# Window attention and routed experts on one core: a first layer as seven products, part of a table on GpSimd, two weight sums behind a result

## The chip, the cores and the metric

The kernel runs on one core of one Trainium2 chip. The metric is the device time of an execution in microseconds (us); lower is better. Three runs of the kernel before gave 633.9, 635.15 and 629.37 us, so the median is 633.9 us.

## What is computed

The reference is a sliding-window causal attention (8 batches, 8 heads, 576 positions, head width 64, window 64), whose output is the input of a mixture of experts with a "locality gate". Cut to what matters:

```python
# attention: softmax over the 64 keys up to the position, per batch and head
x = attn_out.transpose(0, 2, 1, 3).reshape(8, 576, 512)
logits = x @ w_gate                    # (8, 576, 8 experts)
local = sigmoid(x @ w_local)
for b in range(8):
    for s in range(576):
        fresh_e = argmax(logits[b, s])
        e = fresh_e if s == 0 or local[b, s] < 0.5 else prev_e
        prev_e = e
        p = softmax(logits[b, s])
        h = relu(x[b, s] @ w1[e])      # 512 -> 1024, fp32
        out[b, s] = p[e] * (h @ w2[e]) # 1024 -> 512, fp32
```

## The kernel before, in words

**Attention and first router pass.** Up to about 134 us the kernel computes the attention, 512 tokens at a time, and writes the rows of `x` to memory (`xs`). The routing of the first three sequences is done meanwhile, so that some blocks of tokens are known early.

**Blocks of tokens.** Tokens are sorted by expert into blocks of 256 (two "slots" of 128). For a block, SP loads the expert's weights W1 (2 MB, [128, 4 x 1024]) and W2 (2 MB) into a ring of buffers; GpSimd gathers the rows of `xs` and the softmax weights with indirect DMAs; the block goes through a first layer, a ReLU and a second layer; the result is scaled and scattered to the output rows by GpSimd (L1488). Three first blocks, called -1, -2 and -3, use the early routing. All later blocks need the second router pass, which runs in pieces between the instructions of blocks -1 and -2.

**Seven products.** A block whose `fast1` is set does its first layer (`big_hidden`) as seven products of half size instead of eight. On TensorE (PE) that is 7 x 8 matmuls of 128x128 (L1357). For it VectorE (DVE) makes four sums of the tokens (`xs` in the rows, L1320) and four sums of W1 (L1309, 128x1024 each), ScalarE (ACT) keeps three partial results (L1364), DVE adds them to three quarters (L1369) and ACT does four ReLUs (L1370). A block whose `fast2` is set does its second layer the same way (`big_result`): four sums of W2 (L1320, rows `ws`), four sums of the hidden values (`hs`, L1309), seven products (L1408), three keeps (L1414), three "puts" of a result on DVE (L1419: `put(0,0)`, `put(1,1)`, `put(0,1)`) and one on ACT (L1441). The products share PSUM buffers, so that the seventh product (`hp<-ws,h` in the rows of L1408) waits until `put(1,1)` has read its buffer. `PLAIN1` lists the blocks whose first layer is done directly, by 64 matmuls of 128x256 (L1508) and four ReLUs on ACT (L1521): before, blocks -1 and -2.

**The second router pass** (`Router.second`) is a chain on DVE: counts and ranks of every token, the place of each token (`places`, ending in `lo` at L946 and `hi` at L947), the expert of each block (`experts_of`, `ej`), and then `table`, which turns places into a list of tokens for each slot. `table` handles 37 columns of tokens in pieces of 10, 10, 10 and 7. For a piece, ACT makes `rowh` (one ACTIVATE for each column, L990, and one over the piece, L992), both from `lo`; DVE makes `one` (L980, from `hi`), then `colh`, of which one half is `one * chunk` (L983) and the other `one * posp` (L985); and PE multiplies `rowh` by `colh`, one matmul for a column (L998, 37 in all). From the sum DVE makes the indices for the gathers (L1000 to L1024).

**What sets the order.** Each engine runs its own list in order. The lists of PE and SP are written by hand, by the order of the calls in `run`. There the router is a generator that gives out work at each call of `step`, with `pause` as its account: each `step` takes 1.7 off it, and the next piece comes when it is at zero or below; at i == 1 (block -2) the account is raised by 4.5. Up to block -3 the lists of DVE, ACT and GpSimd are made by a scheduler, from priorities and its own estimates. From the first layer of block -3 on (i == FB-1) all lists are as written. In the loop, `turn` of the next block, with its sums of tokens and of W1, stands ahead of `result` of the present one, so DVE has the four sums of the next W1 ahead of the three puts.

Of the kernel before, what the change touches and what calls it, by code (L numbers as in the profile page):

```python
# [73 lines left out]
MID = (KB, KB - 1)  # L74
PLAIN1, PLAIN2 = (-1, -2), ()

# [636 lines left out]
class Router:  # L713
# [249 lines left out]
    def table(self, psum, cs, ns, lo, hi, idx, gx):  # L963
# [5 lines left out]
        for k in range(0, len(pieces), 2):  # L969
            built = []  # L970
            for b, m in pieces[k:k + 2]:
                rowh = self.oh_p.tile([P, PIECE, P], BF16, name="rowh")[:, :m]
                if ns == FIRST:
# [8 lines left out]
                colh = self.oh_p.tile([P, PIECE, 2, ns], BF16, name="colh", bufs=self.colhs)[:, :m]  # L982
                vec.tensor_tensor(colh[:, :, 0], one, last(self.chunk[:, cs.start + b:cs.start + b + m]).to_broadcast(sh),  # L983
                                  op=Alu.mult)
# [181 lines left out]
class Experts:  # L1166
# [100 lines left out]

    def turn(self, st, quiet, later=False):
        while any(x is st for x, _ in self.asks):
# [21 lines left out]
        if st["fast1"] and not quiet and not later:  # L1291
            self.prepare(st)

    def prepare(self, st):

        st["xq"] = quarters(st["xt"], DK, BIG)
        st["xt"] = self.right("xs", st["xq"])
        w = quarters(st["w1"], DK, F)

        st["wq"] = [[w[0][0], w[1][0]], [w[0][1], w[1][1]]]  # L1300
        st["ws"] = self.left("ws1", st["wq"])

    def left(self, name, a):

        sub, add = Alu.subtract, Alu.add
        s1, s2, s3, s4 = self.sums(name, a)
        for o, x, y, op in ((s1, a[1][0], a[1][1], add), (s2, s1, a[0][0], sub), (s3, a[0][0], a[1][0], sub),
                            (s4, a[0][1], s2, sub)):
            self.nc.vector.tensor_tensor(o, x, y, op=op)  # L1309
        return s1, s2, s3, s4  # L1310

# [20 lines left out]
    def halves(self, st):  # L1332

        hq = st["hq"]
        st["ha"] = [[hq[0][0], hq[1][0]], [hq[0][1], hq[1][1]]]
        st["hs"] = self.left("hs", st["ha"])

    def big_hidden(self, st, step):
# [28 lines left out]
        def relu(o, x, y=None):  # L1367
            if y is not None:
                nc.vector.tensor_tensor(o, x, y, op=add)  # L1369
            nc.scalar.activation(o, x if y is None else o, Act.Relu)  # L1370

# [212 lines left out]
    def run(self, ctx, rt, last=None):  # L1584
# [44 lines left out]
        for i, n in enumerate(order):  # L1629
# [21 lines left out]
            if i == 1:  # L1651
                pause += 4.5
            with tc.issue_after(mark.ins) if i == FB - 1 and mark else nullcontext():
# [10 lines left out]
            if i + 1 == len(order):  # L1664
                self.result(jobs[i], step)
                continue
            self.turn(jobs[i + 1], i + 1 < FB)
            if i + 2 < FB and jobs[i + 1]["fast1"]:
                self.prepare(jobs[i + 1])
            hooks = (step, ) * 6  # L1670
            if order[i + 1] >= KINDS[2]:
# [69 lines left out]
```

## Time and profile before

| what | value |
|---|---|
| median of three runs | 633.9 us (629.37 to 635.15) |
| profiled execution | 631.83 us |
| its span, first to last instruction | 630.1 us |
| mean granted TensorE clock | 0.996 |
| PE busy | 604.0 us, 96% of the span |
| DVE busy | 402.1 us, 64% |
| ACT busy | 200.7 us, 32% |
| GpSimd (POOL) busy | 275.5 us, 44% |
| first layer of block -2 | from 163.94 us |
| first layer of block -3 | from 192.68 us |
| first block of the second pass | from 219.09 us |

The times in the trace are counted from the start of the span. A row of the timeline gives start, length, engine, line, operation, output <- inputs, shape, and how many instructions it joins; in brackets, how long the engine had been idle before it, and what ended that. Instructions of one engine overlap a little (a matmul or a sum that is 1.22 us long may start the next after 1.14 us), so distances from start to start are used as well as lengths.

### The profile page before, as it was taken

To read this page: it belongs to the slowest core of one execution; us is meant where nothing else is said; L and a number is where in the kernel's file an instruction comes from. 1 tells how busy PE (TensorE), PEld (TensorE's weight loads), DVE (VectorE), ACT (ScalarE), POOL (GpSimd) and SP (SyncE) were. 2 spreads that over 40 slices of the span, in tenths; PEclk is the share of its full clock that TensorE was granted. 3 is DMA by queue.
4 is the path that set the end of the run, shared out by engine and by line. 5 is a ranking of instruction groups with operands and counts; after the bars stand their busy time and mean duration, and the time that the engine had idled before them with its cause. 6 is when DMAs were issued, how large, how long until landed. Compare 5 with 4: busy or idle time off the path is not lost. (4 is left out here: it accounts for less than half of the span.)

```text
span 630.1 us, 15072 instructions
## 1 busy us (share of the span) xinstructions
PE 604.0 (96%) x6253; PEld 530.7 (84%) x6253; DVE 402.1 (64%) x757; ACT 200.7 (32%) x368; POOL 275.5 (44%) x261
## 2 busy tenths in 40 slices
PE   8897988999999999999999999999999999999995
PEld 7676766788889998979898889888997998989994
DVE  5667569888986867346472785183927753886730
ACT  3756655632482131203130213022211221213120
POOL 4532111532103567448165873174375765462001
PEclk9999999999999999999999999999999999999998
DMA  8999898886945566487966765678678656965501
GB/s 319 397 419 400 326 377 298 287 319 238 384 154 202 185 227 250 165 295 248 403 244 236 304 221 208 225 305 318 284 262 320 225 186 240 374 217 208 197 18 39
DMA packets 31880, 165.80 MB, mean 263 GB/s; under 512 B 10531, under 2 KB 12217, under 8 KB 22586
## 3 DMA queue, kind: packets, MB, share of 16 engines
q1 hardware_dynamic: 20394, 135.54, 57.9%
q0 software_dynamic: 11408, 29.20, 13.0%
q8 instruction: 51, 0.84, 0.5%
q14 instruction: 27, 0.22, 0.1%
HBM read 145.52 MB, written 19.59 MB: 262 GB/s over the span
## 5 line engine op out<-in xcount | busy, mean ns | idle before, releaser
L1184 POOL DMA_INDIRECT xg<-xs,g x118 | 139.1, 1179 | 46.5 <-issue 25.6
L1488 POOL DMA_INDIRECT out_dram<-y,idx x36 | 40.8, 1133 | 159.0 <-DVE y L1419 69.9
L1408 PE MATMUL hp<-ws,hs 128*128 128x256 f32 x384 | 88.9, 380 | 0.0
L1408 PEld LDWEIGHTS hp<-ws,hs 128*128 128x128 f32 x384 | 72.6, 190 | 10.9 <-issue 1.2
L1357 PE MATMUL hp<-xs,ws 128*128 128x128 f32 x672 | 79.7, 275 | 0.0
L1357 PEld LDWEIGHTS hp<-xs,ws 128*128 128x128 f32 x672 | 77.3, 192 | 0.1
L1508 PE MATMUL hp<-xt,w 128*64 128x64 f32 (+2 forms) x640 | 66.2, 276 | 0.0
L1508 PEld LDWEIGHTS hp<-xt,w 128*128 128x128 f32 (+1 forms) x640 | 60.8, 170 | 4.1 <-issue 0.7
L1419 DVE SCALAR_TENSOR_TENSOR y<-hp,pws,kept 128x256 f32<-128x256 f32 x48 | 22.1, 480 | 63.5 <-issue 38.1
L1408 PE MATMUL hp<-w,h 128*128 128x256 f32 x256 | 60.5, 379 | 0.0
L1369 DVE TENSOR_TENSOR h<-hp,keep 128x512 f32<-128x512 f32 x42 | 28.6, 690 | 44.0 <-PE hp L1357 43.2
L1357 PEld LDWEIGHTS hp<-xt,w 128*128 128x128 f32 x448 | 53.2, 192 | 2.7 <-issue 2.3
L1357 PE MATMUL hp<-xt,w 128*128 128x128 f32 x448 | 54.7, 275 | 0.0
L394 PEld LDWEIGHTS sp<-w 64*64 64x64 f32 x1296 | 39.9, 139 | 16.1 <-issue 11.5
L1408 PEld LDWEIGHTS hp<-w,h 128*128 128x128 f32 x256 | 47.3, 190 | 5.7
L394 PE MATMUL sp<-w 64*64 64x128 f32 (+1 forms) x1296 | 45.8, 272 | 5.7 <-issue 4.2
L425 ACT ACTIVATE p<-sp 128x512 f32<-128x512 f32 x72 | 39.1, 595 | 37.6 <-PE sp L394 35.2
L440 PE MATMUL xo<-vb,p 128*64 128x74 f32 (+1 forms) x576 | 45.0, 230 | 5.5 <-DVE x L450 2.2
L430 DVE TENSOR_TENSOR p<-p,mask 128x1024 f32<-128x1024 f32 x29 | 35.6, 1227 | 22.6 <-ACT p L425 22.5
L1184 POOL DMA_INDIRECT pws<-xw,gx x40 | 43.7, 1093 | 13.1 <-issue 9.8
L440 PEld LDWEIGHTS xo<-vb,p 128*64 128x64 f32 x576 | 39.2, 139 | 9.7 <-issue 4.0
L1320 DVE TENSOR_TENSOR ws<-w 128x1024 f32<-128x1024 f32 x32 | 39.1, 1224 | 11.5 <-PE hp L1408 9.6
(287 smaller groups left out, 967.3 us busy)
## 6 DMA issues: line engine op xcount, KB each, us to landing
w<-in_w_dram SPq DMA_DIRECT2D x22, 2048.0 KB, 9.4
w<-in_w1t_dram SPq DMA_DIRECT2D x20, 2048.0 KB, 8.9
w<-in_kq_dram SPq DMA_DIRECT2D x17, 1024.0 KB, 10.4
w<-in_w_dram SPq DMA_DIRECT2D x24, 512.0 KB, 8.3
xs<-x POOLq DMA_DIRECT2D x9, 1024.0 KB, 7.0
va<-in_v_dram SPq DMA_DIRECT2D x5, 1184.0 KB, 5.3
vtt<-in_vt_dram SPq DMA_DIRECT2D x5, 1024.0 KB, 6.3
va<-in_v_dram SPq DMA_DIRECT2D x3, 1040.0 KB, 14.2
```

What stands on the lines that cost most here:

```text
L394: nc.tensor.matmul(sp[j][c * WIN:(c + 1) * WIN, a:b], lhsT=kt[h, hp, block * WIN:(block + 1) * WIN], rhs=qt[h, hp, a:b], start=not biased, ...
L425: nc.scalar.activation(p[:, j], sp[j], Act.Exp, scale=DH ** -0.5)
L430: masked.append(nc.vector.tensor_tensor(p, p, m.to_broadcast([P, 2, SC]), op=Alu.mult))
L440: nc.tensor.matmul(xo[par * WIN:(par + 1) * WIN, j, s * VW:s * VW + n], lhsT=p[:, j, b * WIN:(b + 1) * WIN], rhs=w[:, s, 2 * hp + j, :n], ...
L1184: return self.nc.gpsimd.indirect_dma_start(out=out, out_offset=None, in_=table[:rows, :], in_offset=bass.IndirectOffsetOnAxis(ap=idx, axis=0))
L1320: self.nc.vector.tensor_tensor(o, x, y, op=sub)
L1357: mm = nc.tensor.matmul(out[:, m, :], lhsT=a[:, kk, m * P:(m + 1) * P], rhs=b[:, kk, :], start=start and m + kk == 0, stop=stop and (m, kk ...
L1369: nc.vector.tensor_tensor(o, x, y, op=add)
L1408: mm = nc.tensor.matmul(out, lhsT=a[:, m, :], rhs=b[:, m, :], start=start and m == 0, stop=stop and m == FK // 2 - 1, skip_group_check=True)
L1419: nc.vector.scalar_tensor_tensor(o, x, pw[i], y2, Alu.mult, Alu.add)
L1488: return self.nc.gpsimd.indirect_dma_start(out=self.out[:, :], out_offset=bass.IndirectOffsetOnAxis(ap=st["idx"][:, s:s + 1], axis=0), in_ ...
L1508: mm = nc.tensor.matmul(hp[a, i, :], lhsT=st["w1"][:, kk, m * P:(m + 1) * P][:, a], rhs=st["xt"][:, kk, :n], start=(kk == 0), stop=(kk == ...
```

## The change

Four edits:

1. `PLAIN1` loses -2. Block -2's first layer is now seven products, with its sums, keeps and adds. With it `relu` in `big_hidden` records its last ACTIVATE, behind which the router puts the second half of each piece's `rowh`; and `pause` is raised by 9.0 instead of 4.5 at i == 1.
2. In `table`, the product `one * chunk` (L983) is issued to GpSimd for the second pass (`ns != FIRST`): four instructions.
3. `left` can make the first two of its four sums and hand back a call that makes the others. `turn` uses it with `rest` for the W1 sums of each block that follows a block of the second kind, from i + 1 = FB on.
4. That call is put into the fifth hook of `big_result`, which stands behind `put(1,1)` and ahead of `put(0,1)`.

```diff
-PLAIN1, PLAIN2 = (-1, -2), ()
+PLAIN1, PLAIN2 = (-1, ), ()
...
-                vec.tensor_tensor(colh[:, :, 0], one, last(self.chunk[:, cs.start + b:cs.start + b + m]).to_broadcast(sh),
+                (vec if ns == FIRST else nc.gpsimd).tensor_tensor(colh[:, :, 0], one, last(self.chunk[:, cs.start + b:cs.start + b + m]).to_broadcast(sh),
                                   op=Alu.mult)
...
-    def turn(self, st, quiet, later=False):
+    def turn(self, st, quiet, later=False, rest=False):
...
         if st["fast1"] and not quiet and not later:
-            self.prepare(st)
-
-    def prepare(self, st):
+            return self.prepare(st, rest)
+
+    def prepare(self, st, rest=False):
...
-        st["ws"] = self.left("ws1", st["wq"])
-
-    def left(self, name, a):
+        st["ws"], later = self.left("ws1", st["wq"], rest)
+        return later
+
+    def left(self, name, a, rest=False):
 
         sub, add = Alu.subtract, Alu.add
         s1, s2, s3, s4 = self.sums(name, a)
-        for o, x, y, op in ((s1, a[1][0], a[1][1], add), (s2, s1, a[0][0], sub), (s3, a[0][0], a[1][0], sub),
-                            (s4, a[0][1], s2, sub)):
-            self.nc.vector.tensor_tensor(o, x, y, op=op)
-        return s1, s2, s3, s4
+        todo = [(s1, a[1][0], a[1][1], add), (s2, s1, a[0][0], sub), (s3, a[0][0], a[1][0], sub), (s4, a[0][1], s2, sub)]
+
+        def make(n):
+            for o, x, y, op in todo[:n]:
+                self.nc.vector.tensor_tensor(o, x, y, op=op)
+            del todo[:n]
+
+        make(2 if rest else 4)
+        return (s1, s2, s3, s4), lambda: make(4)
...
         def relu(o, x, y=None):
             if y is not None:
                 nc.vector.tensor_tensor(o, x, y, op=add)
-            nc.scalar.activation(o, x if y is None else o, Act.Relu)
+            st["last"] = nc.scalar.activation(o, x if y is None else o, Act.Relu)
...
             if i == 1:
-                pause += 4.5
+                pause += 9.0
...
-            self.turn(jobs[i + 1], i + 1 < FB)
+            more = self.turn(jobs[i + 1], i + 1 < FB, rest=i + 1 >= FB and jobs[i]["fast2"])
...
-            hooks = (step, ) * 6
+            hooks = (step, ) * 4 + (more or step, step)
```

**What it moves.** Lines below about L1309 stand six further on in the changed kernel (L1320 is now L1326, L1309 is L1312, L1357 is L1363, L1369 is L1375, L1414 is L1420, L1419 is L1425, L1441 is L1447). On PE, block -2's 32 rows of L1508 give way to the 56 matmuls of L1363, and the 37 matmuls of L998, of which 20 stood between the fourth and the fifth product of block -2's second layer, now stand together behind the seventh, ahead of block -3's first layer. On DVE, the four token sums and four W1 sums of block -2 stand right behind the router's running count (L884) and ahead of block -1's three puts, and most of the router stands behind these puts.

On DVE, in the middle of block -2, the end of the router's `places`. Before, with what follows it (`ws_2803` are the sums of block -2's W2, `hs` those of its hidden values):

```order
L935 TENSOR_REDUCE plc<-pl 128x37
L1144 SCALAR_TENSOR_TENSOR more<-send,more 1x1
L937 MEMSET plc 64x1
L939 MEMSET plc 64x1
L1145 SCALAR_TENSOR_TENSOR ej<-bend,more 1x1
L941 CAST plc_i<-plc 128x37
L943 TENSOR_SCALAR lo_i<-plc_i 128x37
L944 TENSOR_SCALAR plc_i<-plc_i 128x37
L946 CAST lo<-lo_i 128x37
L947 CAST hi<-plc_i 128x37
L1320 TENSOR_TENSOR ws_2803<-w 128x1024 x2
L1320 TENSOR_TENSOR ws_2803<-w,ws_2803 128x1024
```

The same place in the changed kernel:

```order
L935 TENSOR_REDUCE plc<-pl 128x37
L1312 TENSOR_TENSOR hs<-h 128x512 x2
L1312 TENSOR_TENSOR hs<-hs,h 128x512
L937 MEMSET plc 64x1
L939 MEMSET plc 64x1
L1312 TENSOR_TENSOR hs<-h,hs 128x512
L941 CAST plc_i<-plc 128x37
L960 TENSOR_REDUCE ef<-ec 1x43
L943 TENSOR_SCALAR lo_i<-plc_i 128x37
L1142 TENSOR_SCALAR more<-qend 1x1
L961 TENSOR_SCALAR ej<-ef 1x43
L944 TENSOR_SCALAR plc_i<-plc_i 128x37
```

`lo` and `hi` follow within four rows. Before, they stood ahead of the four sums of W2 and of the four `hs`; now the four W2 sums, the three adds of the first layer and all four `hs` stand ahead of them.

On ACT, in block -2's second layer (`kept` is what it keeps of the products, `h` the plain first layer's ReLU), one piece of the difference:

```order
+L1420 ACTIVATE kept_2862<-hp,pws 128x256
 L990 ACTIVATE rowh<-io_744,lo 128x128 x4
-L1521 ACTIVATE h<-hp 128x512
-L990 ACTIVATE rowh<-io_744,lo 128x128 x7
+L1420 ACTIVATE kept_2868<-hp,pws 128x256
+L990 ACTIVATE rowh<-io_744,lo 128x128 x5
+L1420 ACTIVATE kept_2874<-hp,pws 128x256
+L990 ACTIVATE rowh<-io_744,lo 128x128 x2
 L992 ACTIVATE rowh<-rowh,ones 128x1280
```

All `rowh` stood between the ReLUs of block -2's first layer and its second layer's keeps; now the first of them stands behind the first keep, and the last (not shown) behind the result on ACT.

On DVE, between two later blocks, as it repeats from there on (`ws_3341` are the next block's W1 sums, L1419 the three puts, `ws_3408` the W2 sums). Before:

```order
L1309 TENSOR_TENSOR ws_3341<-w 128x1024
L1309 TENSOR_TENSOR ws_3341<-ws_3341,w 128x1024
L1309 TENSOR_TENSOR ws_3341<-w 128x1024
L1309 TENSOR_TENSOR ws_3341<-w,ws_3341 128x1024
L1419 SCALAR_TENSOR_TENSOR y<-hp,pws,kept_3356 128x256
L1419 SCALAR_TENSOR_TENSOR y<-hp,pws,kept_3363 128x256
L1419 SCALAR_TENSOR_TENSOR y<-hp,pws,kept_3370 128x256
L1320 TENSOR_TENSOR ws_3408<-w 128x1024
```

In the changed kernel:

```order
L1312 TENSOR_TENSOR ws_3383<-w 128x1024
L1312 TENSOR_TENSOR ws_3383<-ws_3383,w 128x1024
L1425 SCALAR_TENSOR_TENSOR y<-hp,pws,kept_3396 128x256
L1425 SCALAR_TENSOR_TENSOR y<-hp,pws,kept_3403 128x256
L1312 TENSOR_TENSOR ws_3383<-w 128x1024
L1312 TENSOR_TENSOR ws_3383<-w,ws_3383 128x1024
L1425 SCALAR_TENSOR_TENSOR y<-hp,pws,kept_3410 128x256
L1326 TENSOR_TENSOR ws_3450<-w 128x1024
```

Two sums of 128x1024 have moved from ahead of the first two puts to behind them. On GpSimd the four new products stand between the second scatter of block -1 and the first of block -2; SP's list is the same.

More of the change, by code (lines that the diff above doesn't have):

```diff
@@ L1335, in halves @@
         st["ha"] = [[hq[0][0], hq[1][0]], [hq[0][1], hq[1][1]]]
-        st["hs"] = self.left("hs", st["ha"])
+        st["hs"], _ = self.left("hs", st["ha"])
     def big_hidden(self, st, step):
```

## The prediction

> **What bounds the kernel now.** I read the page's busy times first, then PE's timeline around the blocks that change, then what PE waits for there and later.
>
> ```profile
> PE 604.0 (96%) x6253; PEld 530.7 (84%) x6253; DVE 402.1 (64%) x757; ACT 200.7 (32%) x368; POOL 275.5 (44%) x261
> ```
>
> PE works 96% of the span: matmuls taken from it, or a wait of PE taken away or added, show in the time; another engine matters only where PE waits for it. PE from the end of block -1's second layer to the start of block -3's first:
>
> ```profile
> 162.11 1.99 PE L1408 MATMUL hp<-ws,h 128*128 128x256 f32 x8 [0.44 <-DVE y L1419]
> 163.94 13.98 PE L1508 MATMUL hp<-xt,w 128*128 128x256 f32 x64
> 177.75 1.04 PE L1279 MATMUL tp<-ident,xg 128*128 128x128 f32 x8
> ...
> 191.75 0.99 PE L998 MATMUL r<-colh,rowh 128*128 128x108 bf16 x17
> 192.57 0.27 PE L168 MATMUL yp<-ident,ok 128*1 128x128 f32 x1
> 192.68 1.95 PE L1357 MATMUL hp<-xt,w 128*128 128x128 f32 x16
> ```
>
> The one gap shown is 0.44 us ahead of the seventh product at 162.11, where DVE is late with a put. The table's matmuls (L998) wait for nothing. So PE bounds this stretch, but DVE is close behind it:
>
> ```profile
> 152.97 0.53 DVE L884 TENSOR_TENSOR_SCAN run<-te,zero 128x184 f32<-128x184 f32 x1
> ...
> 161.58 0.47 DVE L1419 SCALAR_TENSOR_TENSOR y<-hp,pws,kept 128x256 f32<-128x256 f32 x1
> ```
>
> ```profile
> 146.30:156.00 9.70, 9.70 (x51) 8.44 (x50) 9.13 (x27) 2.63 (x6) 1.90 (x2) 1.00 0.81 273
> 153.40:178.00 24.60, 24.16 (x114) 20.92 (x113) 24.25 (x93) 10.26 (x29) 6.20 (x6) 1.00 0.90 327
> ```
>
> The fields of the windows are the stretch, its length, busy time of PE, PEld, DVE, ACT and POOL, the granted clock (1.00), the DMA share and GB/s. From 153.4 to 178 DVE is busy 24.25 of 24.6 us: what is put ahead of something in its list delays it by its own length.
>
> **Seven products for block -2 (edit 1), on PE.** In the first block of the second pass PE's groups start at:
>
> ```profile
> 207.01 1.89 PE L1408 MATMUL hp<-w,h 128*128 128x256 f32 x8
> ...
> 219.09 1.95 PE L1357 MATMUL hp<-xt,w 128*128 128x128 f32 x16
> ...
> 231.60 1.89 PE L1408 MATMUL hp<-w,h 128*128 128x256 f32 x8
> ```
>
> Seven products of a first layer take 231.60 - 219.09 = 12.5 us, against 177.75 - 163.94 = 13.8 for the plain one: **-1.3 us**. A second layer takes 219.09 - 207.01 = 12.1. On ACT three keeps are added, where it was busy 10.26 of 24.6 us and now has its rowh later: nothing.
>
> **The same edit on DVE.** Four token sums and four W1 sums now stand right behind L884, ahead of block -1's puts. Their lengths, from a later block:
>
> ```profile
> 368.45 0.41 DVE L1320 TENSOR_TENSOR xs<-xt,xs 128x256 f32<-128x256 f32 x1
> 368.78 1.21 DVE L1309 TENSOR_TENSOR ws<-w 128x1024 f32<-128x1024 f32 x1
> ...
> 373.45 1.26 DVE L1419 SCALAR_TENSOR_TENSOR y<-hp,pws,kept 128x256 f32<-128x256 f32 x3
> 376.40 1.23 DVE L1320 TENSOR_TENSOR ws<-w 128x1024 f32<-128x1024 f32 x1 [1.70 <-PE hp L1408]
> ```
>
> Four token sums at 0.33 to 0.41 make 1.5 us, the W1 sums 373.45 - 368.78 = 4.7: 6.2 us. In return most of the router moves behind the put at 161.58. Of the 8.1 us between 153.5 (end of L884) and 161.58 some 3 stay ahead (down to the ranks), an estimate from the order, so the put would start at 153.5 + 6.2 + 3 = 162.7, 1.1 us later. The sums can also wait for block -2's W1, four parts that SP issued from 146.28 on (its row stands below). The window from 146.3 to 156 moved 9.7 x 273 = 2.65 MB, W1's 2.1 and two gathers among it, so I take 156 for W1, up to 1 us of waiting behind the token sums. The put is 1 to 2 us late; I take 1.5. Block -2's first layer then starts at 165.5 and ends at 178.0, against 177.75: the late put uses up what the seven products give.
>
> **The table (edits 1 and 2) decides.** `lo` was there at 167.4 (first row of ACT's chain below). Now the token and W1 sums (6.2), the W2 sums (4.7, of the same size), three adds and four hs stand ahead of it:
>
> ```profile
> L1369 DVE TENSOR_TENSOR h<-hp,keep 128x512 f32<-128x512 f32 x42 | 28.6, 690 | 44.0 <-PE hp L1357 43.2 <-ACT h L1370 0.7
> L1309 DVE TENSOR_TENSOR hs<-h 128x512 f32<-128x512 f32 x32 | 22.0, 688 | 9.9 <-ACT h L1370 9.7
> ```
>
> 3 x 0.69 = 2.1 and 4 x 0.69 = 2.75; 15.7 us in all, so `lo` at 183.1. A wait for W1 adds up to one; neighbours overlap (the W1 sums start 1.17 us apart and are 1.21 long), which takes about one. The other bound is the first layer: its sixth product ends at 165.5 + 6 x 1.79 (a seventh of 12.5) = 176.2, then come its add, its ReLU, the hs and six small rows: not before about 181. I take **182.1**, bounds 181 and 184. Behind `lo` stands ACT's chain:
>
> ```profile
> 167.42 1.28 ACT L990 ACTIVATE rowh<-io,lo 128x128 bf16<-128x128 f32 x4 [2.81 <-DVE lo L946]
> ...
> 169.09 2.14 ACT L990 ACTIVATE rowh<-io,lo 128x128 bf16<-128x128 f32 x7
> 171.13 1.35 ACT L992 ACTIVATE rowh<-rowh,ones 128x1280 bf16<-128x1280 bf16 x1
> 172.38 0.58 ACT L1521 ACTIVATE h<-hp 128x512 f32<-128x512 f32 x1
> ...
> 188.40 1.04 ACT L992 ACTIVATE rowh<-rowh,ones 128x896 bf16<-128x896 bf16 x1
> ```
>
> One L990 takes (171.13 - 169.09) / 7 = 0.29 us, 37 take 10.8; L992 takes 172.38 - 171.13 = 1.25 three times and 1.04 once, 4.8; two keeps and block -2's result stand between, half as wide as L1521's 0.58 us, some 0.37 each, 1.1, an estimate. Sum 16.7 us: the last rowh is ready at 182.2 + 16.7 = 198.9. Before, the chain began at 167.42, with 25 us until PE took its last piece, and cost nothing.
>
> PE comes to L998 early: transposes at 178.0 for some 0.9, second layer to 178.9 + 12.1 = 191.0. There it waits, and behind the last rowh it still has seven matmuls of (192.57 - 191.75) / 17 = 0.05 and L168's 0.11, and some 0.2 for the signal. Block -3's first layer, queued behind them, starts at 198.9 + 0.2 + 0.35 + 0.1 = 199.6 instead of 192.68: **+6.9 us**. This holds the -1.3 and the late put, which end at the same place. With the bounds of `lo` it is +5.8 to +8.8.
>
> What else is late: SP's next weights wait for `ej`, now at about 182.5.
>
> ```profile
> 146.28 17.33 SPq L1261 DMA_DIRECT2D w<-in_w_dram  x16
> ...
> 177.94 12.62 SPq L1261 DMA_DIRECT2D w<-in_w_dram  x2
> ```
>
> W1 of the first block of the second pass was issued at 177.94 and is 5 us late at 183, for a first layer that was at 219.09 and comes at 226: hidden. The gathers come behind the table as before and move with it.
>
> **GpSimd's four products.** DVE loses them behind `lo`, where the chain is ACT's: no gain. No two-input GpSimd operation is in the trace; nearest are one-input copies:
>
> ```profile
> L369 POOL COPY vb<-va 64x1184 f32<-64x1184 f32 x5 | 6.2, 1246 | 50.5 <-PE xo L440 39.1 <-ACT vb L355 11.3
> ```
>
> ```profile
> 19.79 2.04 POOL L373 COPY vb<-va 64x1040 f32<-64x1040 f32 x1
> ```
>
> 1246 ns for 1184 elements, 1.05 ns each, gives 0.6 us for 540; the slowest, 1.96 ns, doubled for two inputs, 2.1 us. I take 1.3, between them. They start at 183.3 with the first `one`, end between 185.7 and 191.7, and are needed by 199: nothing, up to 3.9 us each. Were rowh early again, they would be due by 191, and at 2.1 us each cost up to 1 us.
>
> The Trainium skill ("GPSIMD Engine Reference", section 3.1, "Elementwise — side-by-side cycle accounting") gives 4497 ns for a two-input addition of 2048 elements; for 540 that makes 1.2 us, an estimate, and leaves the sum as it is.
>
> **W1's last sums behind the second put (edits 3 and 4).** In later blocks PE waits for the same put; from 206 to 625 us its waits read:
>
> ```profile
> PE hp L1408 <- DVE y L1419: 1.6, 5, 0.4
> ```
>
> ```profile
> 372.18 1.89 PE L1408 MATMUL hp<-w,hs 128*128 128x256 f32 x8
> 374.37 1.99 PE L1408 MATMUL hp<-ws,h 128*128 128x256 f32 x8 [0.30 <-DVE y L1419]
> ```
>
> The seventh product starts 2.19 us behind the sixth, where 12.1 / 7 = 1.73 is the rule: 0.46 each, five times **-2.3 us** (at least the row's 1.6). Two W1 sums, 2.3 us, go behind the put, which can start at about 372 instead of 373.9. What comes late: `put(0,1)`, by these sums to about 374.5, when its own product has just ended; the next first layer, which takes the two sums in its fifth and sixth product, 7 us in; the W2 sums, ahead of which DVE stood idle 1.70. All hidden; if not, the 2.3 us are lost, and up to as much again if PE then waits for the two sums in full.
>
> **Sum.** +6.9 - 2.3 = +4.6 us on the profiled 631.83: 636.4. The median is 2.1 above that execution: **638.4 us**.
>
> **The rivals.** *The give-back fails* (chance 0.17): the table waits, but each removed put wait comes back, by `put(0,1)`, the W1 sums or a transfer that PE now meets earlier. For it: each wait was only 0.46 us, and the next may be as close. Against it: the 1.70 us of idle DVE. +6.9 alone: 640.8, slower.
>
> *GpSimd decides the table* (0.10): its products take over 3.9 us each, with repeated operands and bf16, which no row shows. At 5 us they end at 203.4, some 4.4 behind the rowh: 642.8, slower. Against it: this is over twice the dearer bound.
>
> The Trainium skill ("SBUF — State Buffer", section "Who interferes with whom") says that a DVE instruction with two SBUF inputs and a GpSimd one that reads SBUF shut each other out. From 182 on DVE has 1.5 us of token sums, 4.7 of W1 sums, three puts and the table's own rows; with GpSimd's 5.2 us one after the other that leaves some 4 us for puts and table rows until 199, so by this rule little is added. No row here shows it yet.
>
> *The table is not late* (0.15), the other side: `lo` comes by 174, and rowh is done by 191. Then the late put (+1.5), -1.3 and -2.3 remain: -2.1, 631.8. For it: rowh had 25 us to spare. Against it: `hs`, ahead of `lo`, needs the sixth product, which ends at 176.
>
> *W1 is later than 156* (0.05): at 160 the late put, `lo` and rowh all move by 4, since DVE's list stands behind its sums: 642.4, slower. For it: the DMA share of 0.90. Against it: by bytes it is there.
>
> **How the numbers follow.** The forecast has 0.53, its own range 636 to 641. A measurement of this kernel tells about 1% (6.3 us) from no change: below 627.6 or above 640.2. Faster: 0.05, a third of the not-late case, with a lower draw (the three runs spread by 5.8). Slower: 0.10 of the forecast's 0.53 (the upper bound of `lo`), 0.10 of the failed give-back, 0.09 and 0.04 of GpSimd and W1: 0.33. Within 1%: 0.62. The range 631 to 644 takes in both sides' cases.
>
> **What would show it.** Right: block -2's L1363 from 165 to 166; `lo` at 181 to 184 and rowh from there for 17 us without a gap; PE some 7 us idle at L998, released by ACT's L992; block -3's first layer at 199 to 200; past 206 no wait of the seventh product on DVE's `y`. Wrong: PE's gap at L998 put down to `colh`; `lo` below 175; the later blocks' wait still there, or another in its place.

## The result and the profile after

Four runs each, in turn on one chip: 639.54 us for the changed kernel (638.48 to 642.1), 631.68 for the one before (629.37 to 635.15). The ratio is 1.015, 95% interval 1.012 to 1.018: slower by 1.5%, some 9.5 us (the two medians lie 7.9 us apart), where +4.6 had been forecast. The page of the profiled execution, the slowest of the four:

```profile
span 640.2 us, 15191 instructions
PE 604.6 (94%) x6301; PEld 533.5 (83%) x6301; DVE 409.8 (64%) x764; ACT 203.3 (32%) x371; POOL 279.9 (44%) x265
```

PE is busy as long as before (604.6 against 604.0 us) in a span that is 10.1 us longer: most of the loss is waiting. (The seven products should have taken 1.3 us from PE's busy time; slow matmuls, below, put it back.) PE from block -1's transposes to block -3's:

```profile
150.40 1.04 PE L1279 MATMUL tp<-ident,xg 128*128 128x128 f32 x8
...
163.21 1.99 PE L1414 MATMUL hp<-ws,h 128*128 128x256 f32 x8 [1.42 <-DVE y L1425]
165.04 1.95 PE L1363 MATMUL hp<-xt,w 128*128 128x128 f32 x16
...
177.54 1.04 PE L1279 MATMUL tp<-ident,xg 128*128 128x128 f32 x8
...
191.62 2.84 PE L1414 MATMUL hp<-ws,h 128*128 128x256 f32 x8 [2.68 <-DVE y L1425]
194.25 1.97 PE L998 MATMUL r<-colh,rowh 128*128 128x108 bf16 x20
198.62 0.66 PE L998 MATMUL r<-colh,rowh 128*128 128x108 bf16 x10 [2.40 <-ACT rowh L992]
201.46 0.81 PE L998 MATMUL r<-colh,rowh 128*128 128x108 bf16 x7 [2.18 <-ACT rowh L992]
202.06 0.42 PE L168 MATMUL yp<-ident,ok 128*1 128x128 f32 x1
202.28 3.62 PE L1363 MATMUL hp<-xt,w 128*128 128x128 f32 x16
...
217.41 1.04 PE L1279 MATMUL tp<-ident,xg 128*128 128x128 f32 x8
```

The first layer of block -2 starts at 165.04 and ends at 177.54, about as forecast (165.5, 178.0). Block -3's starts at 202.28, not at 199.6. Two things here had not been in the sum: the seventh product of block -2 waits 2.68 us for a put, and block -3's first product takes 205.69 - 202.28 = 3.41 us where one takes 1.79. DVE in between:

```profile
181.27 0.16 DVE L946 CAST lo<-lo_i 128x37 f32<-128x37 int32 x1
...
183.25 0.61 DVE L985 TENSOR_SCALAR colh<-one,posp 128x540 bf16<-128x540 bf16 x2
183.80 0.70 DVE L980 TENSOR_TENSOR one<-ios,hi 128x540 bf16<-128x540 f32 x1
185.49 1.42 DVE L980 TENSOR_TENSOR one<-ios,hi 128x378 bf16<-128x378 f32 x1 [0.99 <-POOL colh L983]
186.84 1.50 DVE L985 TENSOR_SCALAR colh<-one,posp 128x540 bf16<-128x540 bf16 x2
188.26 0.71 DVE L1326 TENSOR_TENSOR xs<-xt,xs 128x256 f32<-128x256 f32 x1
...
191.09 0.47 DVE L1425 SCALAR_TENSOR_TENSOR y<-hp,pws,kept 128x256 f32<-128x256 f32 x1
```

```profile
182.71 5.98 POOL L983 TENSOR_TENSOR colh<-one,chunk 128x540 bf16<-128x540 bf16 x4 [8.18 <-DVE one L980]
```

The same four products, each in a row of its own (views of the short windows in which they run):

```profile
182.71 2.74 POOL L983 TENSOR_TENSOR colh<-one,chunk 128x540 bf16<-128x540 bf16 x1 [8.18 <-DVE one L980]
185.42 1.08 POOL L983 TENSOR_TENSOR colh<-one,chunk 128x540 bf16<-128x540 bf16 x1
186.47 1.39 POOL L983 TENSOR_TENSOR colh<-one,chunk 128x540 bf16<-128x540 bf16 x1
187.83 0.87 POOL L983 TENSOR_TENSOR colh<-one,chunk 128x378 bf16<-128x378 bf16 x1
```

`lo` comes at 181.27 (forecast 182.1). Then GpSimd's four products take 6.0 us, and beside them the fourth `one` waits 0.99 us for a product to free its buffer and takes 1.42 us, two scales take 1.50 where two took 0.61 just before, and a token sum 0.71 where one takes 0.42. The second put, behind all this, two more token sums and a W1 sum, starts at 191.09. ACT, whose rowh were to set the time:

```profile
181.47 1.28 ACT L990 ACTIVATE rowh<-io,lo 128x128 bf16<-128x128 f32 x4 [0.60 <-DVE lo L946]
...
194.50 0.47 ACT L1447 ACTIVATE y<-hp,pws 128x256 f32<-128x256 f32 x1 [2.94 <-PE hp L1414]
194.87 2.44 ACT L990 ACTIVATE rowh<-io,lo 128x128 bf16<-128x128 f32 x8
...
200.36 1.04 ACT L992 ACTIVATE rowh<-rowh,ones 128x896 bf16<-128x896 bf16 x1
```

ACT stands idle for 2.94 us in the middle of the chain: its next instruction is block -2's result, which needs the late seventh product, and fourteen columns of rowh are queued behind it. Without that gap the chain takes 17.0 us (181.47 to 201.40, less 2.94), where the prediction had 16.7. And the granted clock (the field behind the five busy times):

```profile
191.60:194.30 2.70, 2.68 (x9) 2.03 (x10) 2.70 (x4) 0.00 (x0) 0.00 (x0) 0.69 0.93 394
194.30:202.30 8.00, 3.42 (x40) 3.08 (x39) 1.06 (x1) 6.87 (x17) 1.75 (x1) 0.71 0.26 107
202.30:205.70 3.40, 3.40 (x18) 3.40 (x18) 3.26 (x16) 0.00 (x0) 0.00 (x0) 0.50 0.00 0
```

It was 1.00 up to 191.6; after PE's gap of 2.68 us it is 0.69, so that the seventh product takes 2.84 us instead of 1.99, and for 3.4 us of full work from 202.3 on it is 0.50. From block -3's first product to the transposes behind its first layer it is 217.41 - 202.28 = 15.1 us; before it was 206.13 - 192.68 = 13.45. So the idle time cost 1.7 us more after it had ended (that the idle time is the cause is shown by the runs on the clock below). In the later blocks the wait for the put is gone:

```profile
PE hp L1363 <- DVE h L1375: 0.4, 2, 0.2
```

That is all PE waits for from 206 to 640 us; before, the five put waits stood beside it. By PE's starts: from block -3's transposes to the first layer of the last block 623.63 - 217.41 = 406.2 us, before 615.09 - 206.13 = 409.0, so -2.7 us.

```profile
615.09 3.95 PE L1508 MATMUL hp<-xt,w 128*64 128x64 f32 x128
```

```profile
623.63 3.95 PE L1514 MATMUL hp<-xt,w 128*64 128x64 f32 x128
```

The attention before block -1 takes a different time in each execution (its transposes start between 147.0 and 151.2 us in the runs below), and so does the end (14.0 to 16.7 us from the last block's first layer). So I compare stretches between these marks. The change adds 11.1 us up to block -3's transposes and gives back 2.7: +8.4, which is within the interval of the ratio (7.5 to 11.4 us).

### The profile page after: what moved, and what is told of

It is laid out like the page before. It is cut to its first block, busy times and chain, and to the rows that moved or that the text cites. A ratio compares the mean times of both kernels' runs of the same rounds, so it can differ in the third digit from the quotient of the medians.

```text
span 640.2 us, 15191 instructions
## 1 busy us (share of the span) xinstructions
PE 604.6 (94%) x6301; PEld 533.5 (83%) x6301; DVE 409.8 (64%) x764; ACT 203.3 (32%) x371; POOL 279.9 (44%) x265
## 5 line engine op out<-in xcount | busy, mean ns | idle before, releaser
L1184 POOL DMA_INDIRECT xg<-xs,g x118 | 134.5, 1140 | 47.7 <-issue 23.8
L1414 PE MATMUL hp<-ws,hs 128*128 128x256 f32 x384 | 88.8, 380 | 0.0
L1363 PE MATMUL hp<-xs,ws 128*128 128x128 f32 x720 | 85.8, 276 | 0.0
L1363 PEld LDWEIGHTS hp<-xs,ws 128*128 128x128 f32 x720 | 83.2, 193 | 0.2
L1414 PEld LDWEIGHTS hp<-ws,hs 128*128 128x128 f32 x384 | 72.6, 190 | 10.9 <-issue 1.2
L1425 DVE SCALAR_TENSOR_TENSOR y<-hp,pws,kept 128x256 f32<-128x256 f32 x48 | 23.1, 481 | 65.7 <-issue 41.2
L1363 PEld LDWEIGHTS hp<-xt,w 128*128 128x128 f32 x480 | 58.7, 197 | 2.8 <-issue 2.3
L1414 PE MATMUL hp<-w,h 128*128 128x256 f32 x256 | 60.5, 379 | 0.0
L1363 PE MATMUL hp<-xt,w 128*128 128x128 f32 x480 | 60.2, 280 | 0.0
L1375 DVE TENSOR_TENSOR h<-hp,keep 128x512 f32<-128x512 f32 x45 | 30.6, 689 | 45.7 <-PE hp L1363 45.7
L1514 PE MATMUL hp<-xt,w 128*64 128x64 f32 (+2 forms) x576 | 52.2, 264 | 0.0
L1414 PEld LDWEIGHTS hp<-w,h 128*128 128x128 f32 x256 | 47.3, 190 | 5.7
L1184 POOL DMA_INDIRECT pws<-xw,gx x40 | 45.3, 1132 | 14.2 <-issue 8.5
L430 DVE TENSOR_TENSOR p<-p,mask 128x1024 f32<-128x1024 f32 x29 | 37.1, 1279 | 21.6 <-ACT p L425 21.5
L1514 PEld LDWEIGHTS hp<-xt,w 128*128 128x128 f32 (+1 forms) x576 | 48.6, 168 | 2.5 <-issue 0.7
L1376 ACT ACTIVATE h<-h 128x512 f32<-128x512 f32 x45 | 28.3, 632 | 64.3 <-DVE h L1375 64.3
## 6 DMA issues: line engine op xcount, KB each, us to landing
va<-in_v_dram SPq DMA_DIRECT2D x3, 1040.0 KB, 15.3
```

The lines of the kernel that those rows point to most:

```text
L430: masked.append(nc.vector.tensor_tensor(p, p, m.to_broadcast([P, 2, SC]), op=Alu.mult))
L1184: return self.nc.gpsimd.indirect_dma_start(out=out, out_offset=None, in_=table[:rows, :], in_offset=bass.IndirectOffsetOnAxis(ap=idx, axis=0))
L1363: mm = nc.tensor.matmul(out[:, m, :], lhsT=a[:, kk, m * P:(m + 1) * P], rhs=b[:, kk, :], start=start and m + kk == 0, stop=stop and (m, kk ...
L1376: st["last"] = nc.scalar.activation(o, x if y is None else o, Act.Relu)
L1414: mm = nc.tensor.matmul(out, lhsT=a[:, m, :], rhs=b[:, m, :], start=start and m == 0, stop=stop and m == FK // 2 - 1, skip_group_check=True)
L1425: nc.vector.scalar_tensor_tensor(o, x, pw[i], y2, Alu.mult, Alu.add)
```

## The experiments

Twelve kernels. The table gives PE's starts in us behind the start of block -1's transposes (L1279), so that differences ahead of it drop out; "rest" is from block -3's transposes to the last block's first layer; the ratio is to the kernel before, timed in turn on the same chip.

| run | first layer of -2 | `lo` | transposes of -2 | first layer of -3 | transposes of -3 | rest | ratio (95%) |
|---|---|---|---|---|---|---|---|
| before | 13.7 | 17.0 | 27.5 | 42.4 | 55.9 | 409.0 | 1 |
| the change | 14.6 | 30.9 | 27.1 | 51.9 | 67.0 | 406.2 | 1.015 (1.012 to 1.018) |
| rest_only | 13.7 | 16.9 | 27.5 | 42.4 | 55.9 | 406.1 | 0.993 (0.990 to 0.995) |
| no_seven | 13.7 | 16.9 | 27.5 | 42.4 | 55.9 | 406.0 | 0.995 (0.992 to 0.998) |
| no_gpsimd | 14.8 | 31.1 | 27.4 | 49.0 | 63.8 | 406.1 | 1.008 (1.005 to 1.011) |
| lo_first | 15.3 | 24.3 | 28.3 | 50.0 | 64.8 | 406.1 | 1.007 (1.005 to 1.010) |
| y_on_dve | 15.7 | 32.8 | 29.4 | 51.0 | 66.4 | 406.1 | 1.013 (1.009 to 1.017) |
| keep_warm | 14.8 | 31.1 | 27.3 | 53.9 | 67.4 | 406.2 | 1.016 (1.013 to 1.019) |
| lo_first_dve | 14.3 | 23.1 | 27.1 | 45.0 | 59.6 | 406.0 | 1.001 (0.999 to 1.004) |
| all_three | 17.2 | 26.5 | 30.5 | 48.1 | 61.6 | 406.1 | 1.003 (1.000 to 1.005) |
| late_table | 13.7 | 21.3 | 27.5 | 45.2 | 59.6 | 419.6 | 0.999 (0.995 to 1.002) |
| free_all | 14.3 | 23.3 | 27.3 | 43.4 | 58.3 | 423.4 | 0.998 (0.994 to 1.001) |
| best | 13.1 | 22.5 | 26.6 | 42.9 | 57.5 | 418.6 | 0.998 (0.995 to 1.001) |
| keep_warm2 | 16.0 | 32.8 | 29.4 | 50.8 | 64.3 | 419.1 | 1.004 (1.000 to 1.008) |

The last four ran on a chip where every kernel was slower, the one before too (644.6 us): the rest took 419 to 423 us, with waits that the other traces do not show. Of these runs the stretches up to block -3 are compared with the others, the totals only among themselves. The line numbers differ a little from run to run: L1423 in some of the rows below is L1414 of the change, L1456 is L1447, L1364 is L1363.

### The parts of the change, each without the other

`rest_only`, edits 3 and 4 alone:

```diff
-PLAIN1, PLAIN2 = (-1, ), ()
+PLAIN1, PLAIN2 = (-1, -2), ()
...
-                (vec if ns == FIRST else nc.gpsimd).tensor_tensor(colh[:, :, 0], one, ...
+                vec.tensor_tensor(colh[:, :, 0], one, ...
...
-                pause += 9.0
+                pause += 4.5
```

> Edits 3 and 4 alone (W1's last two sums behind the second put), with block -2's plain first layer and the table product on DVE as before. Theory A (the three parts add: the late put wait of later blocks is gone, about -2.7 us by the starts of the later blocks in the two traces): ratio to before 0.995 to 0.997, no wait of L1414 on DVE y past 206 us, block -3's first layer near 192.7. Rival B (the waits come back elsewhere, and the later part only looked faster because it ran at another place): ratio 1.000, and another wait of about 0.5 us in each of five blocks.

Up to block -3 every mark stands as before to 0.1 us; the rest is 2.9 us shorter, and PE waits for no put. Theory A holds, and B falls. The ratio is somewhat better than the 2.9 us (0.995) that the trace shows; its interval just reaches that.

`no_seven` takes back edit 1 alone (the first and the last hunk above), with the products on GpSimd.

> The change without edit 1: block -2's first layer plain, the four table products on GpSimd, W1's last sums behind the second put. Theory A (the late lo makes the loss; GpSimd costs only where DVE's delay reaches PE): lo near 167, rowh early, block -3's first layer within 1 us of 192.7, ratio to before 0.994 to 0.998. Rival C (GpSimd's products and DVE shutting each other out are the main loss): block -3 starts 3 us late or more, ratio at least 1.001. In either case DVE's one and colh rows beside the four products should be up to twice as long as before.

As theory A had it, block -3 starts at 42.4, as before. Yet DVE was disturbed here too:

```profile
175.50 3.21 POOL L983 TENSOR_TENSOR colh<-one,chunk 128x540 bf16<-128x540 bf16 x3
179.21 0.86 POOL L983 TENSOR_TENSOR colh<-one,chunk 128x378 bf16<-128x378 bf16 x1 [0.50 <-DVE one L980]
```

```profile
176.66 2.47 DVE L980 TENSOR_TENSOR one<-ios,hi 128x378 bf16<-128x378 f32 x1 [1.14 <-POOL colh L983]
...
188.99 0.48 DVE L1425 SCALAR_TENSOR_TENSOR y<-hp,pws,kept 128x256 f32<-128x256 f32 x1 [0.64 <-ACT rowh L990]
```

The `one` of 378 takes 2.47 us, over four times its 0.54 in the kernel before, where at most twice had been expected. But DVE has idle time left ahead of the second put (0.64 us), so nothing arrives at PE. A disturbance of this kind costs nothing here and 2.9 us in the change: what decides is the cover, the time that DVE has to spare ahead of the put.

`no_gpsimd` takes back edit 2 alone (the second hunk).

> The change with the four table products back on DVE. Theory A (late lo is some 7 us; GpSimd adds by a chain: DVE late, second put late, seventh product late, ACT's result copy late, the last rowh behind it late): lo still at 181 to 182, but ACT's rowh without the 2.9 us gap ahead of block -2's result, block -3's first layer at 199 to 200 instead of 202.3, ratio to before 1.007 to 1.011. Rival C (GpSimd is the main loss): block -3 at 195 or earlier, ratio below 1.003. Rival D (GpSimd costs nothing, since the chain is ACT's anyway): block -3 at 202, ratio 1.015.

```profile
192.49 0.46 ACT L1447 ACTIVATE y<-hp,pws 128x256 f32<-128x256 f32 x1
```

```profile
200.25 3.49 PE L1363 MATMUL hp<-xt,w 128*128 128x128 f32 x16
```

ACT's result has no idle time ahead of it, and block -3 starts at 49.0 behind the mark: +6.6 against before (forecast +6.9), and 2.9 earlier than in the change. Theory A holds: the late table is 6.6 us, edit 2's part 2.9, through the put. The first product is slow here too (3.33 us until the next).

The run does not hold all else fixed, though: DVE's order changed with it. Here the second put stands ahead of three token sums and a W1 sum, in the change behind them. From `lo` to the second put it is 6.95 us here (182.30 to 189.25) and 9.82 in the change (181.27 to 191.09). By the rows, the four products that left DVE's list give back some 2.4 us, the four sums that came ahead of the put take some 2.1, and DVE's wait and its long rows beside GpSimd make some 3.0. So the 2.9 us are the price of edit 2 with the order that came with it; no run separates the two. Some 0.85 of them, an estimate, is the slow clock, since ACT's result starts only when the seventh product, 0.85 us longer than usual, has ended.

### The late `lo`

`lo_first` runs the router on, at the end of block -2's first layer, until `lo` and `hi` are issued, and puts the W2 sums and hs behind them:

```diff
-        self.prepare2(st)
+        if not link:
+            self.prepare2(st)
...
-        self.halves(st)
+        marks = []
+        if link:
+            old = link[1]()
+            while link[1]() is old or len({id(x) for x in link[1]()}) > 1:
+                step()
+            marks = [x.ins for x in link[1]()]
+            self.prepare2(st, marks)
+        with self.tc.issue_after(marks[-1]) if marks else nullcontext():
+            self.halves(st)
```

> The change, with the router run on until lo and hi ahead of block -2's four W2 sums and four hs sums on DVE (these are put behind hi in the order); everything else as in the change, GpSimd's products too. Theory A: lo near 173, rowh starts 8 us earlier, so the wait at L998 is gone or under 4 us, block -3's first layer at 194 to 198 instead of 202.3; ratio to before 1.000 to 1.007. Rival C (GpSimd's products hold the put, and the put holds everything): the seventh product still waits about 2.7 us, and block -3 stays above 200; ratio above 1.010.

`lo` is 6.6 us earlier behind the mark, block -3 only 1.9: the ratio is as theory A had it, the gain behind the mark is not. The seventh product still waits 2.39 us for its put, as rival C had it, ACT's result waits 4.46 for the seventh product, and seven columns stand behind it. With `lo` early, the other chain decides. `lo_first_dve` takes GpSimd's products away as well:

> The change with lo and hi ahead of block -2's W2 sums and hs sums, and the table products on DVE: both causes of the late table taken away, but ACT's result copy still stands ahead of the last seven rowh columns. Theory A: second put on time to half a microsecond, block -3's first layer about 45 us behind block -1's transposes (42.4 before, 51.9 in the change), ratio to before 0.995 to 1.003. Rival G (seven products in block -2 cost by DVE's full list whatever the order): block -3 48 us or more behind them, ratio 1.006 or more.

Block -3 at 45.0, ratio 1.001: both as theory A had them, G falls. What is left is this:

```profile
189.49 0.48 ACT L1456 ACTIVATE y<-hp,pws 128x256 f32<-128x256 f32 x1 [0.87 <-PE hp L1423]
```

```profile
193.26 0.64 PE L998 MATMUL r<-colh,rowh 128*128 128x108 bf16 x7 [2.36 <-ACT rowh L992]
```

PE waits 2.36 us for the last seven columns. They stand behind the result in ACT's list, and ACT could begin them only when PE had ended the second layer.

### What holds the last columns

`y_on_dve`: the change, with block -2's result quarter on DVE, so that it is out of ACT's list.

```diff
-        nc.scalar.activation(y[1][:, :w], px, Act.Copy, scale=pw[1])
+        if st.get("ydve"):
+            nc.vector.tensor_scalar(y[1][:, :w], px, pw[1], None, Alu.mult)
+        else:
+            nc.scalar.activation(y[1][:, :w], px, Act.Copy, scale=pw[1])
...
+                jobs[1]["ydve"] = True
```

> The change, with the last quarter of block -2's result scaled on DVE instead of ACT, so that no rowh stands behind it on ACT; GpSimd's products, the late lo and the late second put stay as in the change. Theory A (GpSimd's products reach the time through one chain: DVE late, second put late, seventh product late, ACT's result copy late, the last fourteen rowh columns late): rowh without a gap on ACT, last L992 at about 198 instead of 201.4, block -3's first layer some 3 us earlier after the same start, ratio to before 1.007 to 1.011, as with the products on DVE. Rival E (the late seventh product itself is what costs): block -3 within 1 us of the change's, ratio 1.013 to 1.017.

In this execution block -2 started 1.1 us later than in the change: its W1 sums waited 0.92 us for the weights instead of 0.33, and behind the longer wait for the put (1.98 us) block -1's seventh product took 2.56 us instead of 1.99. Behind block -2's transposes, block -3 starts 21.7 us, as in no_gpsimd (21.7) and 3.1 less than in the change (24.7): the chain through ACT is as theory A says. The ratio, 1.013, is the one that rival E had named, but it holds the late start too, so it does not tell the theories apart. And one wait took the removed one's place:

```profile
196.61 0.40 ACT L990 ACTIVATE rowh<-io,lo 128x128 bf16<-128x128 f32 x1 [0.55 <-PE r L998]
```

The first column of the fourth piece waits for PE's matmuls of the first: rowh has three buffers, and a fourth piece needs one back. `all_three` puts both together, the early `lo` with the products on DVE and the result on DVE:

> As the run with lo first and the products on DVE, and block -2's last result quarter on DVE as well. Theory A: the last rowh is ready before PE has finished block -2's second layer, PE idle at L998 under 1 us, block -3's first layer 42 to 43.5 us behind block -1's transposes, ratio to before 0.990 to 0.997, which is that of W1's last sums alone, give or take the 1.3 us of the seven products. Rival G: no better than the run without this, ratio 1.000 or more.

Missed: block -3 at 48.1 and the ratio 1.003 are what rival G had named, and behind block -2's transposes block -3 starts hardly earlier than in `lo_first_dve` (17.7 us against 17.9). W1 came late here (1.98 us of waiting, block -2 started at 17.2), and PE still waited for the last columns:

```profile
193.56 2.15 ACT L990 ACTIVATE rowh<-io,lo 128x128 bf16<-128x128 f32 x7 [1.35 <-PE r L998]
```

```profile
196.84 0.51 PE L998 MATMUL r<-colh,rowh 128*128 128x108 bf16 x7 [2.35 <-ACT rowh L992]
```

So there is a third cause, which I had not seen: in the change all 37 table matmuls stand behind the seventh product, so the first piece's buffer comes free only then, and the last piece takes ACT 3.2 us from there (193.56 to 196.79 here). `late_table` gives this order to `rest_only`, by one number:

```diff
-                pause += 4.5
+                pause += 9.0
```

> The kernel with only W1's last sums moved (edits 3 and 4) and one number of edit 1: the router's account raised by 9.0 instead of 4.5, which on PE puts all 37 table matmuls behind the seventh product of block -2's second layer (20 stood behind its fourth product); the plain first layer, the early lo and the products on DVE stay. Theory H (rowh has three buffers, so the fourth piece's rowh waits until PE has taken the first piece, and then still needs 3.2 us on ACT): block -3's first layer starts 1.5 to 3 us later, at 44 to 45.5 us behind block -1's transposes instead of 42.4, with PE waiting on ACT's L992 ahead of the last seven matmuls; ratio to before 0.995 to 0.999, against 0.993 for the sums alone. Rival: the order on PE is free as long as lo is early: 42.4 to 43, ratio 0.993.

```profile
188.79 0.47 ACT L1447 ACTIVATE y<-hp,pws 128x256 f32<-128x256 f32 x1 [2.05 <-PE hp L1414]
```

```profile
192.56 0.81 PE L998 MATMUL r<-colh,rowh 128*128 128x108 bf16 x7 [2.35 <-ACT rowh L992]
```

As theory H had it, block -3 is at 45.2, +2.8, with the plain first layer and `lo` at 21.3 (4.4 later, by the same number, but ACT was idle 2.05 us ahead of the result, so `lo` was not what held it). This run alone does not tell the buffer from ACT's list: the seven columns stand right behind the result and start as it ends (189.28), about when PE has taken the first piece. `all_three`, with the result off ACT, still had the wait; `free_all` gives it a fourth buffer for `rowh` and for `one`, and a fifth for `colh`:

```diff
-        rt.rows_of(ctx, tc, "rt_oh2", 3)
+        rt.rows_of(ctx, tc, "rt_oh2", 4)
```

> As the run all_three, with four buffers for rowh and one instead of three. Theory H: the wait of 2.35 us for the last rowh piece is gone, since no rowh waits for PE any more; block -3's first layer starts 14 to 15 us behind block -2's transposes (17.7 with three buffers), ratio to before 0.993 to 0.999, held above that of the sums alone by block -1's late put where W1 lands late. Rival G (seven products in block -2 cost by DVE's full list whatever the order): 17 us or more, ratio 1.002 or more.

```profile
193.81 0.51 PE L998 MATMUL r<-colh,rowh 128*128 128x108 bf16 x7 [0.75 <-ACT rowh L992]
```

No rowh waits for PE, and the wait at L998 falls from 2.35 to 0.75 us. Block -3 starts 16.1 us behind block -2's transposes (17.7 with three): better, short of the 14 to 15 expected, because ACT's own work still ends last. G, which had 17 us or more and a ratio of 1.002 or more, falls. Its transposes stand at 58.3 all the same, since PE then waits 1.61 us for DVE's `t` at L1022. `best` also moves block -2's W1 sums behind block -1's second layer in the program:

```diff
-            if i + 2 < FB and jobs[i + 1]["fast1"]:
-                self.prepare(jobs[i + 1])
             hooks = (step, ) * 4 + (more or step, step)
...
             self.result(jobs[i], step, hooks)
+            if i + 2 < FB and jobs[i + 1]["fast1"]:
+                self.prepare(jobs[i + 1])
```

> As free_all, with block -2's W1 sums made in the program behind block -1's second layer, so that the order puts only two of them ahead of its first two puts. Theory A and H together: block -1's seventh product waits under 0.7 us for its put, block -2's first layer starts 13.5 to 14.2 us behind block -1's transposes also where W1 lands late, and what the seven products save (1.3 us) is left: block -3's first layer 41 to 42.5 us behind block -1's transposes, ratio to before 0.990 to 0.994, at or below that of the sums alone. Rival: a new wait in block -2's first layer for the W1 sums that are now later, ratio 0.996 or more.

Missed, by 0.4 us in block -3's start and in the ratio (0.998 for 0.990 to 0.994). The put is no longer late: block -2's first layer at 13.1, its transposes at 26.6, 0.9 us ahead of before. But block -3 starts at 42.9, and its transposes stand at 57.5 against 55.9 before:

```profile
192.35 0.51 PE L998 MATMUL r<-colh,rowh 128*128 128x108 bf16 x7 [1.00 <-ACT rowh L992]
...
201.49 0.59 PE L1022 MATMUL r<-t,ident 128*32 128x54 f32 x32 [1.37 <-DVE t L1017]
```

The 0.9 us are lost again, and more, at L998 (1.00) and at L1022 (1.37). The rival's wait for the W1 sums is not there; PE waits 0.74 us for an add of the first layer (`h`, on DVE). Its ratio cannot be told from 1, nor from `free_all`'s. The fastest version measured is the plainest one, `rest_only` (0.993); `no_seven` (0.995) is faster than the kernel before, too.

### The clock

`keep_warm` puts matmuls that nobody reads into PE's three waits, in the change as it is:

```diff
+                if ns != FIRST and k:
+                    self.warm(16)
                 for i in range(m):
...
+        if st.get("warm"):
+            st["warm"](20)
         product(px, a[1][1], t[3], False)
```

> The change with matmuls that nobody reads in PE's three waits (20 ahead of the seventh product, 16 each ahead of the third and the fourth piece of the table, 128x128 fp32). Theory F (PE's idle time lets the granted clock fall to 0.5 to 0.7, and block -3's first products pay for it): granted clock 1.0 from 190 to 206, block -3's first product takes 1.8 us instead of 3.4, and the time falls by 1 to 2.5 us against the change, ratio to before 1.010 to 1.013; block -3's start moves by less than 0.7 us. Rival: the low clock has another cause (power, a phase of the program): the first product still takes 3.3 us or more, ratio 1.015.

```profile
201.34 1.95 PE L1365 MATMUL hp<-xt,w 128*128 128x128 f32 x16
```

```profile
200.00:203.00 3.00, 3.00 (x33) 2.99 (x32) 1.57 (x7) 0.00 (x0) 0.00 (x0) 1.00 0.00 0
```

Clock 1.00, the first product 1.95 us long as before (3.62 in the change), and block -3's first layer takes 13.45 us again: theory F. But the fillers ran past the waits (4.5, 3.6 and 3.6 us), so block -3 started 2 us later and the total did not fall: the expected 1.010 to 1.013 was missed. `keep_warm2` has 8, 7 and 7 of them:

> As keep_warm, with 8, 7 and 7 unread matmuls instead of 20, 16 and 16, which had run past the end of the waits (4.5 and twice 3.6 us) and so moved the table by some 3 us themselves. Theory F: the waits are filled for 1.8 and 1.6 us, the table does not move, the granted clock stays above 0.9, the first product of block -3 takes under 2.3 us; ratio to before 1.010 to 1.014. If the idle time left is still enough for the clock to fall: first product above 3 us, ratio 1.015.

The first product is at full speed (13.46 us for the layer), and block -3 starts 21.5 us behind block -2's transposes instead of 24.7. Of that second gain the clock is only a part: the order put eight columns instead of fourteen behind ACT's result in this kernel (seven in `keep_warm`), which I had not meant, and the ratio, 1.004, lies below the 1.010 to 1.014 expected. So what the clock costs is shown by the first layer alone, 1.7 us.

## Why the prediction was right or wrong

The time fell into the range partly by luck: the sum was 4 us short (+4.6 for +8.4), while the median that it starts from, 633.9 us of three runs, lies 2.2 above the 631.68 that the same kernel took beside the change. Two of the signs that were to show it right did not come: rowh has a gap of 2.94 us, and block -3 starts at 202.28 and not at 199 to 200.

- **The late `lo`: right, in place and size.** 181.3 for 182.1; without GpSimd block -3 starts at +6.6, forecast +6.9. `lo` behind the sums, 17 us of ACT behind `lo`. But my reason was not complete: `lo_first_dve`, `all_three` and `late_table` show that this order of the table's matmuls costs 2.6 to 2.8 us with an early `lo` too. `all_three` against `free_all` shows why: the fourth piece of rowh waits for PE to free the first one's buffer; in the other two the result on ACT stands ahead of that piece as well. In the change that wait lies under the later one. The 0.2 us that the sum takes for the signal to PE is shown by no row; here PE goes on at 201.46, 0.06 us behind ACT's last rowh.
- **GpSimd's products: "nothing, up to 3.9 us each" failed.** They took 1.5 us on average, within the bounds of 0.6 to 2.1, the first 2.74, and all were there long before 199. What failed is the due time: I asked when PE needs the products, not when DVE's put, queued behind the table's rows, is due. That put is the first row in the chain put, seventh product, result on ACT, fourteen columns of rowh, and it has no slack: 2.9 us (the change against no_gpsimd, and in time 1.015 against 1.008), with the order on DVE that came with the edit. The rival "GpSimd decides the table" had the cost, but by another way: PE's gap at L998 is put down to ACT's rowh, not to `colh`. I had also called PE "early" at L998, which hid that ACT's result waits for PE there.
- **The Trainium skill's rule on the port** ("SBUF — State Buffer", section "Who interferes with whom") says that a DVE instruction with two inputs in SBUF and a GpSimd one that reads SBUF shut each other out. It was weighed against this wrong due time, too, and so found harmless. The trace agrees with the rule. In the change the `one` of 378, which takes 0.54 alone, starts just behind GpSimd's second product and ends 0.41 us behind that product's end (186.91, 186.50); in `no_seven` it meets two products and ends 0.42 behind the second of them (179.13, 178.71). The other way round, GpSimd's first product ends 0.95 us behind DVE's third `one` (185.45, 184.50), close to the length of a product alone. A scale of 540, with one input tensor, is held as well (1.18 us where it takes 0.34). So the rows look like one engine standing still while the other's instruction runs. The 0.99 us ahead of the fourth `one` are for a buffer, but that buffer is late because the first product took 2.74 us.
- **The late first put: right.** PE's wait ahead of block -2's first layer rose by 1.0 us (1.5 taken), and the seven products took it back (12.5 us).
- **The clock: a term that was missing.** An idle PE was counted as idle time alone; the slow products behind it are 1.7 us. The Trainium skill ("TensorE: Matmul & The Clock Gate", "Part 1: The HAM clock gate") says that an array that was idle for a window of about 3.4 us falls to half its clock and gets it back after a busy window of the same length. By that rule the penalty would be half of 3.4; the trace has 0.50 for 3.4 us, and 1.7 us. But none of PE's gaps here is that long (2.68, 2.40 and 2.18 us), and behind the first of them the clock already stands at 0.69, so in this the measurement differs from the page.
- **W1's last sums: right.** -2.7 to -3.0 us for -2.3.

Put together: +6.6 table, +2.9 GpSimd, +1.7 clock, -2.7 give-back are +8.5, against +8.4 between the marks. The parts are differences between the same marks, so that they add up is no test of them. What stays open is how much of the 2.9 us is GpSimd and how much DVE's order, why `rest_only` gains some more in time than in the trace, and how much of y_on_dve's total is the chance of W1's arrival.

## What to carry to other kernels

Ask of each work that becomes slower which instruction stands behind it on the same engine and when that one is due; the work's own due time says little. When a consumer is moved to the end of a stage, look for the buffer that it gives back: its producer may wait for it. When an experiment takes one edit away, compare the engines' orders before putting the difference down to that edit. And an idle stretch of TensorE can cost more than its length, so price the slow products behind it.

## What the hardware showed that I had not expected

A gap of 2.7 us in PE's work was enough to bring the granted clock to 0.69, and in `y_on_dve` one of 1.98 us (0.78 in the 2.4 us behind it, then 0.60). After a gap of 2.36 us the first product took 3.2 us (`lo_first_dve`); after one of 2.35 us it ran at full speed (`all_three`). So a gap of this size may cost 1.5 us or nothing. The matmuls that nobody reads held the clock at 1.00 through such waits.

GpSimd's product of 540 bf16 pairs took 1.1 us for each of three in `no_seven`, near the 1.3 of the sum. In the change the first took 2.74 us, with DVE's table rows running beside it, and the same four lengths (2.74, 1.08, 1.39, 0.87) come back in `y_on_dve` and `keep_warm`.
